# The first of six triangular inverses, made of two blocks of 16 steps joined by small TensorE products

## The chip, the cores and the metric

The program runs on one core of a Trainium2 chip. The metric is the device time in microseconds of one execution, lower is better. Five engines work side by side, each through its own list of instructions: TensorE (PE), VectorE (DVE), ScalarE (ACT), GpSimd (POOL) and SyncE (SP), which here issues all DMAs. They wait for one another through semaphores.

## The reference

```python
# attention: B, H, S, D = 4, 8, 768, 40; state is (B, H, D, D), from zero
for t in range(S):
    y[:, :, t] = einsum('bhd,bhde->bhe', rt, state)
    Sa = einsum('bhde,bhe->bhd', state, at)
    state = state * wt[:, :, None, :] - einsum('bhd,bhe->bhde', Sa, bt) + einsum('bhd,bhe->bhde', vt, kt)
# x = y as (3072, 320); then two dense layers
h = x @ w_in;  solu = h * softmax(h);  ln = (solu - mean) / sqrt(var + 1e-06) * g_ln   # 1024 wide
x = ln @ w_out
h = x @ w_in2; g = max(h, 0) + alpha * min(h, 0);  out = g @ w_out2                  # 2048 wide
```

All in float32. The recurrence is the serial part: each step of the state needs the state before.

## The kernel before

**Tiling.** The 768 time steps are cut into 12 windows of 64 (w) and 24 groups of 32 (g). The 32 heads (4 x 8) lie in the free dimension and in bands of 32 partitions. Inside a group the recurrence is written as matrices: a 32x32 strictly lower matrix L for every head says how each step's correction Sa depends on the earlier ones, and solving for all 32 steps means multiplying with the inverse of a unit lower triangular matrix made of L. One inverse serves four groups (two windows), so there are six; each handles 128 matrices: 4 groups x 32 heads. In the inverse a partition is one matrix's place: the 128 partitions hold four blocks of 32 lanes, and the free dimension holds the 32x32 matrix.

**Phase 1** (`phase1`, line 917). First windows 0 and 1 are loaded and prepared (`prep_load`, `prep_scan`, `prep_kb`, `prep_a`: running products of w on VectorE, applied to k, b, a), and `gen1` (line 314) makes the matrices on TensorE: VectorE copies one half of each PSUM result into XS (line 336), ScalarE copies the other half, negated, into `lraw` (line 339). Then `init` clears tiles on POOL, `load_g(0)` loads the first group, and the first inverse runs alone (lines 941 to 945). After that come 24 slots, one for each group (`slot`, line 844).

**The inverse** (`inverse`, line 343) turns `lraw` into NT by a VectorE transpose of 32x32 blocks (line 366), then takes 31 steps. Step s adds the outer product of column s of L with row s of the result: a product into tmp (line 354) and a sum into M (line 358). In the first inverse VectorE takes the first 10 rows, in two parts, and POOL the rest (`PR`, line 33). A last transpose (line 387) gives NT, which the stages u and uf use as weights. The five later inverses are cut into pieces and put between the other work of the slots (`inv_tasks`, `invs`).

**A slot** runs on TensorE in a written order: `stage_x` (px), then `stage_u` (pu, needs NT), `stage_uf` (pf), `stage_st` (pst; its result goes back to VUS by VectorE, line 482), `stage_g2`, `stage_s` (pss; line 508), `stage_y`, and between them the generation of the next windows, transposes of kbf (`trans`) and pieces of the dense layers. The other engines' order is not written by hand: the framework plans it ahead of time from program order and planned times. `dec` puts the decoding of weight words (`decode`, lines 656 to 665, and the split in lines 692 and 693) behind the last recorded "fence" instruction. The fence is the inverse's last transpose until `stage_st` records its own. Slot 0 decodes the six pieces of the first dense layer.

**Keeping TensorE busy.** `keep(n)` (line 209) issues n products of 128x512 whose result nobody uses. `pace` is called after each little set of products; it counts columns issued lately by planned times, and when the count falls under a floor it puts keep-busy products in until it stands above the floor by a margin. Before the first slot's u stage there are 24 of them at once (`KEEP1`); they wait for one VectorE memset on their operand that is issued after step `KSTEP` of the first inverse.

**SP** issues all loads in one order: the windows, mask, ident, kbf, then the group's tiles (whose targets POOL clears first), window 2, and the first weight words.

Of the kernel before, what the change touches and what calls it, by code (L numbers as in the profile page):

```python
# [7 lines left out]
F32 = mybir.dt.float32  # L8
# [10 lines left out]
WIN = 64  # L19
SPAN = 3.413  # L20
LEVELS = ((3500, 1300), (3100, 1300), (3100, 1300), (3100, 1300))
KEEP0, KEEP1, KSTEP, KEND = 36, 24, 20, 4
PTR, PT0 = (9, 10, 12, 13), (14, 14, 15, 15)
WT = {(0, 'gen00'): 0.44, (0, 'gen20'): 1.8, (0, 'tr1'): 0.19, (0, 'x'): 9.9, (0, 'y'): 0.62, (1, 'tr3'): 2.59, (1, 'u'): 1.48, (1, 'x'): 0.72, (1, 'y'): 1.54, (2, 'tr1'): 0.12, (2, 'u'): 1.34, (3, 'tr3'): 0.38, (3, 'u'): 0.52, (3, 'x'): 0.32, (4, 'tr0'): 0.2, (4, 'tr1'): 0.6, (4, 'u'): 2.76, (5, 'gen30'): 0.32, (5, 'tr3'): 0.38, (5, 'u'): 2.12, (5, 'x'): 0.59, (5, 'y'): 0.25, (6, 'tr0'): 0.2, (6, 'tr1'): 0.58, (6, 'u'): 1.32, (7, 'tr3'): 0.78, (7, 'u'): 0.84, (8, 'tr0'): 0.2, (8, 'tr1'): 0.58, (8, 'u'): 1.28, (9, 'tr3'): 0.9, (9, 'u'): 1.19, (10, 'u'): 2.57, (11, 'u'): 1.09}
VS, NC, NL = 0, (2, 3, 1, 0), (3, 3, 3, 0)
# [21 lines left out]

@with_exitstack
def tile_kernel(ctx: ExitStack, tc: tile.TileContext, w_fm, a0_fm, a_fm, kb_fm, r_fm, v_fm, v_tm,
                w1_in, w1_out, g_ln, w2_in, w2_out, alpha, ident_d, mask_d, r, k, v, w, a, b, w1_nat, out,  # L50
                manual=True):
    nc = tc.nc
    NW = w_fm.shape[0]
# [55 lines left out]
    KBP = [ca.tile([128, 1280], F32, name=f"KBS{i}") for i in range(3)]  # L109
    KBS = [t.rearrange("p (e s d) -> p e s d", e=2, d=D) for t in KBP]  # L110
    XP = ca.tile([128, 320], F32, name="XP")
    LMN = [lm.tile([128, 32, 32], F32, name=f"LMN{i}") for i in range(3)]
    VUS = [ca.tile([128, 2, 16, 40], F32, name=f"VUS{i}") for i in range(2)]
    VUF = [ca.tile([104, 16, 2, 32], F32, name=f"VUF{i}") for i in range(2)]
# [16 lines left out]
    def unit(M, eng):  # L131
        eng.memset(M, 0.0)
        eng.memset(M.rearrange("p a b -> p (a b)")[:, ::33], -1.0)

    def init():
        unit(LMN[0], nc.gpsimd)
        for t in YS:
            nc.gpsimd.memset(t[32:64, 1], 0.0)
            nc.gpsimd.memset(t[0:64, 0], 0.0)
            nc.gpsimd.memset(t[64:128, 1], 0.0)  # L140
        for t in VUS:
            nc.gpsimd.memset(t[32:64, 0], 0.0)
            nc.gpsimd.memset(t[32:64, 1], 0.0)
        for t in VUF:
            nc.gpsimd.memset(t[32:64], 0.0)
        for t in KBS:
            nc.gpsimd.memset(t[32:64, 0], 0.0)
            nc.gpsimd.memset(t[96:128, 1, 0], 0.0)
        for t, i in ((VUS[0], 0), (KBS[0], 1)):
            nc.gpsimd.memset(t[64:128, i], 0.0)  # L150
            nc.gpsimd.memset(t[0:32, 1 - i], 0.0)
        nc.gpsimd.memset(ebias, -float(896 << 23))
        nc.gpsimd.memset(half, -0.5)
        nc.gpsimd.memset(one, 1.0)
# [159 lines left out]
    def gen1(g, half):  # L314
        w, c = divmod(g, 2)
        x = XS[g % 6]
        kbf = st[w]["kbf"]
        if half == 0:
            st["pg1"] = ps_at.tile([128, 8, 2, 32], F32, name="pg", tag="at")
        pg = st["pg1"]  # L320
        wait(st["slot"], "gen%d%d" % (g % 4, half))
        for p in range(half * 4, half * 4 + 4):
            for pe in range(2):
                for i in range(2):
                    o = 64 * pe + 32 * i
                    nc.tensor.matmul(pg[o:o + 32, p], lhsT=kbf[:, pe * 8 + p, c, i, :], rhs=x[0:104, :, pe, p, :],  # L326
                                     start=True, stop=True)
            pace(0.19, 188)
        if half == 0:
            return  # L330
        c4, lraw = g % 4, st["lraw"]
        for e in range(2):
            q = 64 * e
            for pe in range(2):
                o = 64 * pe
                nc.vector.tensor_tensor(out=x[q:q + 32, e, pe], in0=pg[o:o + 32, :, e],
                                        in1=mask[o:o + 32].unsqueeze(1).to_broadcast([32, 8, 32]), op=ALU.mult)
                r = q + 32 * pe
                nc.scalar.activation(out=lraw[r:r + 32, c4 * 8:c4 * 8 + 8, :], in_=pg[o + 32:o + 64, :, e],
                                     func=AF.Copy, scale=-1.0)  # L340


    def inverse(W):
        M, NT = LMN[2 * W % 3], LMN[(2 * W + 1) % 3]

        P = PR[W > 0]

        def rank1(eng, tmp, s, rows):
            nt = 31 - s
            l = NT[:, s + 1:32, s]  # L350
            tv = tmp[:, 0:sum(b - a for a, b in rows) * nt].rearrange("p (i t) -> p i t", t=nt)
            for a, b in rows:
                sh = [128, b - a, nt]
                eng.tensor_tensor(out=tv[:, a - rows[0][0]:b - rows[0][0]], in0=M[:, a:b, s:s + 1].to_broadcast(sh),  # L354
                                  in1=l.unsqueeze(1).to_broadcast(sh), op=ALU.mult)
            for a, b in rows:
                o = M[:, a:b, s + 1:32]
                r = eng.tensor_tensor(out=o, in0=o, in1=tv[:, a - rows[0][0]:b - rows[0][0]], op=ALU.add)  # L358
            return r

        def pool_rows():
            for s in range(P, 31):
                rank1(nc.gpsimd, b1.tile([128, TM], F32, name="tmp2", tag="Yt"), s, [(P, s + 1)])

        def start():
            nc.vector.transpose(out=NT, in_=st["lraw", W].rearrange("p l t -> p t l"))
            if W:
                unit(M, nc.gpsimd)
            pool_rows()

        def step(s):
            n, nt = min(s + 1, P), 31 - s
            m = n // 2
            if n <= SM:
                ops = [(M[:, i, s + 1:32], NT[:, s + 1:32, s], M[:, i, s:s + 1]) for i in range(n)]
            elif nt <= SM:
                ops = [(M[:, 0:n, s + 1 + i], M[:, 0:n, s], NT[:, s + 1 + i, s:s + 1]) for i in range(nt)]
            else:
                st["step"] = rank1(nc.vector, b1.tile([128, 256], F32, name="tmp"), s,
                                   [(0, m), (m, n)] if W == 0 else [(0, n)])  # L380
                return
            for o, x, f in ops:
                st["step"] = nc.vector.scalar_tensor_tensor(out=o, in0=x, scalar=f, in1=o, op0=ALU.mult,
                                                            op1=ALU.add)

        def fin():
            st["fence"] = nc.vector.transpose(out=NT.rearrange("p l t -> p t l"), in_=M.rearrange("p i t -> p t i"))
            st["NT", W] = NT

        yield 1.1, start  # L390
        for s in range(31):
            yield 0.15 + 2 * (s + 1) * (31 - s) / 960.0, (lambda s=s: step(s))
        yield 1.1, fin

    def trans(w, q):
        kbf = st[w]["kbf"]
# [345 lines left out]

    def gen_tasks(w):
        t = [lambda g=g, h=h: gen1(g, h) for g in (2 * w, 2 * w + 1) for h in range(2)]
        if w % 2 == 0:
            first = t[0]
            t[0] = lambda: (new_l(w // 2), first())
        return t

    def new_l(W):  # L750
        st["lraw"] = st["lraw", W] = LMN[2 * W % 3 if W else 2]

    def fill_tasks(g):

# [89 lines left out]
    def slot(g):  # L844
# [33 lines left out]
        if g == 0:  # L878
            st["busy"] = st["idle"]
            keep(KEEP1)  # L880
        stage_u(g)
        nd = (ND if g < 4 else NL if g >= NG - 4 else NC)[g % 4]
        invs(0.2)
# [33 lines left out]
    def phase1():  # L917
        nc.gpsimd.memset(busy, 0.0)
        st["busy"] = ps_w.tile([128, 512], F32, name="busy", tag="w")
        keep(KEEP0)  # L920
        st["slot"] = 0
        init_scan()
        t0, t1 = vec_tasks(0), vec_tasks(1)
        for f in t0[:3]:
            f()
        nc.sync.dma_start(out=mask, in_=mask_d)
        nc.sync.dma_start(out=ident, in_=ident_d)
        for f in t0[3:] + gen_tasks(0) + t1 + gen_tasks(1):
            f()
        with tc.issue_after(st["kb1"].ins):  # L930
            init()
        busy_t = st.pop("busy")
        for q in range(4):
            trans(0, q)
        load_g(0)
        if NW > 2:
            prep_load(2)
            load_a(4)
            load_a(5)
            kb_load(2)  # L940
        for i, (_, f) in enumerate(inverse(0)):
            f()
            if i == KSTEP:
                with tc.issue_after(st["step"].ins):
                    nc.vector.memset(busy[:, 0:1], 0.0)  # L945
        st["idle"] = busy_t
        nc.sync.dma_start(out=gl, in_=g_ln)
        for g in range(NG):
            if g == KEND:
                del st["busy"]  # L950
            slot(g)
        while wts:
            wts.pop(0)()
# [295 lines left out]
    with ExitStack() as ms:  # L1249
# [8 lines left out]


_INS = ['w_fm', 'a0_fm', 'a_fm', 'kb_fm', 'r_fm', 'v_fm', 'v_tm', 'w1_in', 'w1_out', 'g_ln', 'w2_in', 'w2_out', 'alpha',  # L1260
        'ident', 'mask', 'r', 'k', 'v', 'w', 'a', 'b', 'w1_nat']


def _layout(inputs):
# [56 lines left out]
    o['alpha'] = np.asarray(inputs['moe2_alpha']).reshape(-1, 128).T  # L1321
    o['ident'] = np.eye(128, dtype=f32)
    o['mask'] = (np.arange(32)[None, :] > (np.arange(128) % 32)[:, None]).astype(f32)
    for n in 'rkvwab':
        o[n] = np.asarray(inputs[n])
    o['w1_nat'] = words(np.asarray(inputs['moe_w_in']))
# [22 lines left out]
```

## Time and profile before

| | |
|---|---|
| median of 3 runs | 1167.23 us (1165.36 to 1168.53) |
| the profiled execution | 1166.42 us |
| its span in the profile | 1164.6 us |
| PE busy | 978.9 us, 84% |
| DVE busy | 811.2 us, 70% |
| ACT busy | 520.4 us, 45% |
| POOL busy | 503.7 us, 43% |
| share of the chain that ended last | PE 47%, DVE 29%, POOL 7% |

Times in the profile count from the start of the span. Busy shares are averages: up to about 760 us the slots of the recurrence run and VectorE is the busiest engine in most stretches, after that the second dense layer runs on TensorE alone.

### The profile page before, as it was taken

How to read it: one execution, taken by the hardware profiler on the slowest of the kernel's cores; microseconds unless marked ns; L12 is line 12 of the kernel's file. 1: busy time of each engine (PE TensorE's matmuls, PEld its weight loads, DVE VectorE, ACT ScalarE, POOL GpSimd, SP SyncE). 2: the span in 40 equal slices, each digit the busy share in tenths (PEclk: the TensorE clock that was granted, in tenths of full speed). 3: DMA queues.
4: the chain of work that ended last, by engine and by line, in shares of the span. 5: the costliest groups of instructions: out<-in, count | busy, mean ns of one | idle time of the engine just before them, and what ended most of it. 6: DMA issues, size and time to landing. Idle time of an engine off the chain costs nothing.

```text
span 1164.6 us, 37097 instructions
## 1 busy us (share of the span) xinstructions
PE 978.9 (84%) x15934; PEld 808.5 (69%) x15934; DVE 811.2 (70%) x1610; ACT 520.4 (45%) x1198; POOL 503.7 (43%) x546
## 2 busy tenths in 40 slices
PE   7275687588878978888787878889999999999997
PEld 3143354467666767666676667778989999999997
DVE  8898689978997798779977976656533333333343
ACT  3325454476537653755475547556312121212121
POOL 6858455444434442443344234436233333333333
PEclk8687987789888887988888889999999999999999
DMA  7513343334333433343333342443402020201000
GB/s 161 149 53 85 99 137 113 99 104 120 106 97 107 122 80 96 90 100 111 99 85 88 101 135 71 117 141 133 124 2 61 8 62 7 62 6 41 6 23 15
DMA packets 104543, 99.52 MB, mean 85 GB/s; under 512 B 38068, under 2 KB 83764, under 8 KB 104372
## 3 DMA queue, kind: packets, MB, share of 16 engines
q1 hardware_dynamic: 104372, 97.07, 30.6%
q8 instruction: 127, 2.08, 0.8%
q14 instruction: 44, 0.36, 0.1%
HBM read 71.62 MB, written 25.43 MB: 83 GB/s over the span
## 4 chain that ended last, share of the span: by engine, by line
PE 47%; DVE 29%; POOL 7%; issue 6%; ACT 5%; DMA 5%; SPq 0%; POOLq 0%; DVEq 0%; ACTq 0%
PE ph L1015 15%; DVE tmp L354 5%; PE h L575 5%; PE acc L1035 5%; PE acc L1033 5%; PE acc L1034 5%; DVE LMN L358 4%; DMA kbf<-in_kb_fm_dram 4%; DVE VUS L482 2%; DVE KBS L508 2%; PE pf L465 2%; POOL XS L312 2%; DVE H L277 2%; PE po L628 1%; PE pu L442 1%
## 5 line engine op out<-in xcount | busy, mean ns | idle before, releaser
L1022 POOL TENSOR_TENSOR gll<-gt,gh 128x512 fp32r<-128x512 f32 (+1 forms) x112 | 129.0, 1152 | 224.0 <-ACT gh L1021 222.9
L595 DVE TENSOR_SCALAR gt<-ph,al 128x512 f32<-128x512 f32 (+1 forms) x112 | 75.4, 673 | 189.8 <-PE ph L1015 189.6
L1021 ACT CAST gh<-gt 128x512 fp32r<-128x512 f32 (+1 forms) x112 | 62.5, 559 | 254.5 <-DVE gt L596 212.6
L575 PE MATMUL h<-w1h,xt 128*128 128x512 f32 x240 | 105.2, 487 | 16.3 <-ACT h L584 16.3
L312 POOL TENSOR_TENSOR XS<-XS,H 40x512 f32<-40x512 f32 (+1 forms) x48 | 66.6, 1392 | 92.7 <-DVE H L277 55.8
L354 DVE TENSOR_TENSOR tmp<-LMN,LMN 128x87 f32<-128x87 f32 (+25 forms) x189 | 95.0, 514 | 3.4
L1033 PE MATMUL acc<-w2h,gh 128*128 128x320 f32 x288 | 89.0, 309 | 0.0
L1034 PE MATMUL acc<-w2l,gh 128*128 128x320 f32 x288 | 89.0, 309 | 0.0
L1035 PE MATMUL acc<-w2h,gll 128*128 128x320 f32 x288 | 88.9, 309 | 0.0
L528 POOL TENSOR_TENSOR YS<-YS,mask 64x512 f32<-64x512 f32 x48 | 64.0, 1333 | 49.0 <-ACT YS L527 47.2
L211 PE MATMUL busy<-busy 128*128 128x512 bf16 x221 | 66.4, 455 | 19.5 <-DVE busy L945 18.2
L358 DVE TENSOR_TENSOR LMN<-LMN,tmp 128x87 f32<-128x87 f32 (+25 forms) x189 | 76.3, 415 | 2.7
L596 DVE SCALAR_TENSOR_TENSOR gt<-ph,gt 128x512 f32<-128x512 f32 (+1 forms) x112 | 68.8, 615 | 3.7
L575 PE MATMUL h<-w1l,xt 128*128 128x512 f32 x144 | 68.6, 476 | 0.0
L575 PEld LDWEIGHTS h<-w1h,xt 128*128 128x128 f32 x240 | 50.3, 221 | 26.0 <-ACT h L584 18.5
L628 PE MATMUL po<-wo1h,lnh 128*128 128x320 f32 x192 | 67.1, 349 | 0.5 <-DVE lnl L620 0.5
L630 PE MATMUL po<-wo1h,lnl 128*128 128x320 f32 x192 | 61.9, 322 | 0.0
L629 PE MATMUL po<-wo1l,lnh 128*128 128x320 f32 x192 | 61.8, 322 | 0.0
L1015 PE MATMUL ph<-w1h,w2h 128*128 128x512 f32 x180 | 59.3, 394 | 0.0
L211 PEld LDWEIGHTS <-busy 128*128 128x128 bf16 x221 | 22.9, 112 | 49.7 <-DVE busy L945 18.3
L326 PE MATMUL pg<-XS,kbf 104*32 104x64 f32 x1536 | 38.5, 239 | 22.0 <-DVE kbf L303 12.8
L581 ACT ACTIVATE P<-h,sm 128x1024 f32<-128x1024 f32 x24 | 26.7, 1114 | 65.1 <-DVE sm L580 62.1
(200 smaller groups left out, 2743.5 us busy)
## 6 DMA issues: line engine op xcount, KB each, us to landing
kbf<-in_kb_fm_dram SPq DMA_DIRECT2D x24, 416.0 KB
x2d<-x SPq DMA_DIRECT2D x24, 320.0 KB
xd<-Y SPq DMA_DIRECT2D x24, 256.0 KB
xt<-xd SPq DMA_DIRECT2D x12, 512.0 KB
raw<-in_w_in_dram SPq DMA_DIRECT2D x20, 256.0 KB
wt<-in_w_fm_dram SPq DMA_DIRECT2D x24, 211.7 KB
raw<-in_w_in_dram SPq DMA_DIRECT2D x8, 512.0 KB
raw<-in_w_out_dram SPq DMA_DIRECT2D x16, 256.0 KB
```

Source lines behind the costliest of these rows:

```text
L211: nc.tensor.matmul(st["busy"], lhsT=busy[:, 0:128], rhs=busy, start=True, stop=True)
L312: (nc.vector if w < 2 and e in DA else nc.gpsimd).tensor_tensor(out=o, in0=o, in1=h, op=ALU.mult)
L354: eng.tensor_tensor(out=tv[:, a - rows[0][0]:b - rows[0][0]], in0=M[:, a:b, s:s + 1].to_broadcast(sh), in1=l.unsqueeze(1).to_broadcast(sh) ...
L358: r = eng.tensor_tensor(out=o, in0=o, in1=tv[:, a - rows[0][0]:b - rows[0][0]], op=ALU.add)
L575: nc.tensor.matmul(st["h"][:, ns], lhsT=l, rhs=r, start=j == 0, stop=j == len(ops) - 1)
L595: nc.vector.tensor_scalar(out=tmp, in0=h, scalar1=0.0, scalar2=al, op0=ALU.min, op1=ALU.mult)
L628: nc.tensor.matmul(po, lhsT=lh[:, k], rhs=wo1h[:, k], start=k == 0, stop=False)
L1015: nc.tensor.matmul(p, lhsT=l, rhs=r, start=j == 0, stop=j == len(ops) - 1)
L1022: nc.gpsimd.tensor_tensor(out=gll, in0=t, in1=f32(gh), op=ALU.subtract)
L1033: nc.tensor.matmul(acc, lhsT=gh[:, cs], rhs=oh, start=f == 0, stop=False)
L1034: nc.tensor.matmul(acc, lhsT=gh[:, cs], rhs=ol, start=False, stop=False)
L1035: nc.tensor.matmul(acc, lhsT=gll[:, cs], rhs=oh, start=False, stop=f == K2 - 1)
```

## The change

The first inverse is made in another way. With 16x16 blocks, a lower triangular matrix's inverse has the inverses of the two diagonal blocks on its diagonal, and below them a product of three: second inverse, lower left block, first inverse. Both diagonal blocks are inverted side by side in one set of 14 steps, with all 128 partitions as before (VectorE alone, none on POOL). Then TensorE makes the lower left block: `left` multiplies the block with the first inverse, `join` with the second and puts the parts together, one product of 16 or 32 rows for each of the 128 matrices in each (256 products); ScalarE copies between. `join` writes NT for the first four groups. The products stand in slot 0 on TensorE, after the 24 keep-busy products and before stage u, each set of four followed by a call of `pace`.

ScalarE now writes the matrices of the first four groups to GR, columns in reversed order. POOL's `init` no longer clears M of the first inverse but copies three small constants, which come with a triangle in one new input of 128x321. The keep-busy products' memset is issued after step 2, not 20. `dynamic_dma_scratch_size` is set to 1024 and makes room for the new tiles. The last instruction on VectorE of the new inverse, the transpose into VT, is the new fence.

```diff
-KEEP0, KEEP1, KSTEP, KEND = 36, 24, 20, 4
+KEEP0, KEEP1, KSTEP, KEND = 36, 24, 2, 4
...
+    GR = ca.tile([128, 32, 48], F32, name="GR")
+    VR = ca.tile([128, 32, 32], F32, name="VR")
+    VT = ca.tile([128, 32, 16], F32, name="VT")
+    tri = ca.tile([128, 321], F32, name="tri")
...
     def init():
-        unit(LMN[0], nc.gpsimd)
+        for t, c, k in ((GR, 0, 0), (VR, 0, 1), (LMN[2], 16, 2)):
+            i = tri[:, 256 + 16 * k:272 + 16 * k].unsqueeze(1).to_broadcast([128, 32, 16])
+            nc.gpsimd.tensor_copy(out=t[:, :, c:c + 16], in_=i)
...
-                nc.scalar.activation(out=lraw[r:r + 32, c4 * 8:c4 * 8 + 8, :], in_=pg[o + 32:o + 64, :, e],
-                                     func=AF.Copy, scale=-1.0)
+                to = (GR[r:r + 32, c4 * 8:c4 * 8 + 8, 47:15:-1] if g < 4 else
+                      st["lraw"][r:r + 32, c4 * 8:c4 * 8 + 8, :])
+                nc.scalar.activation(out=to, in_=pg[o + 32:o + 64, :, e], func=AF.Copy, scale=-1.0)
...
+    def first_inverse():
+        X, F = LMN[0], LMN[1]
+        L = X[:, 0:16, :].rearrange("p t (b a) -> p b t a", b=2)
+        A = LMN[2]
+        box = {}
+
+        def start():
+            nc.vector.transpose(out=X[:, 15::-1, :], in_=GR[:, :, 32:48].rearrange("p l c -> p c l"))
+            nc.vector.transpose(out=X[:, ::-1, 16:32].rearrange("p s c -> p c s"),
+                                in_=GR[:, :, 16:32].rearrange("p l c -> p c l"))
+
+        def step(s):
+            sh = [128, 2, 15 - s, s]
+            tmp = b1.tile([128, 256], F32, name="tmp")[:, 0:2 * s * (15 - s)]
+            tmp = tmp.rearrange("p (b t a) -> p b t a", b=2, a=s)
+            nc.vector.tensor_tensor(out=tmp, in0=L[:, :, s + 1:16, s:s + 1].to_broadcast(sh),
+                                    in1=L[:, :, s:s + 1, 0:s].to_broadcast(sh), op=ALU.mult)
+            o = L[:, :, s + 1:16, 0:s]
+            st["step"] = nc.vector.tensor_tensor(out=o, in0=o, in1=tmp, op=ALU.add)
+
+        def fin():
+            V = b1.tile([128, 32, 16], F32, name="V", tag="Yt")
+            low = tri[:, 0:256].rearrange("p (t a) -> p t a", a=16).unsqueeze(1).to_broadcast([128, 2, 16, 16])
+            nc.vector.tensor_tensor(out=V.rearrange("p (b t) a -> p b t a", b=2), in0=L, in1=low, op=ALU.mult)
+            nc.vector.memset(V.rearrange("p (b t) a -> p b (t a)", b=2)[:, :, ::17], 1.0)
+            st["fence"] = nc.vector.transpose(out=VT.rearrange("p l a -> p a l"), in_=V.rearrange("p x a -> p a x"))
+            nc.scalar.activation(out=VR[:, :, 31:15:-1], in_=VT, func=AF.Identity, scale=tri[:, 320:321])
+
+        def units(p, lhsT, rhs, rows, ls):
+            for l in ls:
+                for q in range(0, 128, 32):
+                    nc.tensor.matmul(p[q:q + 32, l - ls[0], :], lhsT=lhsT[q:q + rows, l, 0:32], rhs=rhs[q:q + rows, l, :],
+                                     start=True, stop=True)
+                pace(0.042, 16)
+
+        def left(h):
+            if h == 0:
+                box["p"] = ps_at.tile([128, 32, 16], F32, name="pv", tag="at")
+            p = box["p"]
+            units(p[:, 16 * h:16 * h + 16], GR, VT, 16, range(16 * h, 16 * h + 16))
+            if h:
+                nc.scalar.copy(out=A[:, :, 0:16], in_=p)
+
+        def join(h):
+            ls = range(16 * h, 16 * h + 16)
+            p = ps_at.tile([128, 16, 32], F32, name="pn", tag="at")
+            units(p, A, VR, 32, ls)
+            nc.scalar.copy(out=F[:, 16 * h:16 * h + 16, :], in_=p)
+            st["NT", 0] = F
+
+        yield start
+        for s in range(1, 15):
+            yield lambda s=s: step(s)
+        yield fin
+        for f in (left, join):
+            for h in range(2):
+                yield lambda f=f, h=h: f(h)
...
             keep(KEEP1)
+            for f in st["joins"]:
+                f()
         stage_u(g)
...
         nc.sync.dma_start(out=mask, in_=mask_d)
+        nc.sync.dma_start(out=tri, in_=tri_d)
         nc.sync.dma_start(out=ident, in_=ident_d)
...
-        for i, (_, f) in enumerate(inverse(0)):
+        inv = list(first_inverse())
+        st["joins"] = inv[16:]
+        for i, f in enumerate(inv[:16]):
             f()
...
-    nc = _bacc.Bacc("TRN2", target_bir_lowering=False, num_devices=1)
+    nc = _bacc.Bacc("TRN2", target_bir_lowering=False, num_devices=1, dynamic_dma_scratch_size=1024)
```

## Rows read from the trace of the kernel before

**Rows 1.** Stretches: start:end, length, busy us (count) by engine, PEclk, DMA share, GB/s.
```profile
36.00:59.00 23.00, 1.55 (x64) 1.27 (x65) 22.15 (x78) 6.32 (x20) 20.10 (x48) 0.57 0.54 137
68.00:112.00 44.00, 26.73 (x624) 16.51 (x626) 42.88 (x62) 20.07 (x46) 30.89 (x20) 0.79 0.29 83
200.00:400.00 200.00, 159.85 (x3867) 128.46 (x3867) 172.13 (x354) 118.10 (x285) 86.44 (x98) 0.86 0.41 107
```
**Rows 2.** The chain that ended last, 0 to 200 us: start, length, what.
```profile
65.97 2.03 DVE LMN L387
...
120.71 7.58 DMA kbf<-in_kb_fm_dram
```
**Rows 3.** Timeline of VectorE: start, length, line, operation, tiles, shapes, count.
```profile
25.43 0.69 DVE L303 TENSOR_TENSOR kbf<-kbf,F 104x512 f32<-104x512 f32 x1
...
36.13 1.92 DVE L366 STREAM_TRANSPOSE LMN<-LMN 128x1024 f32<-128x1024 f32 x1 [1.19 <-ACT LMN L339]
...
67.85 0.42 DVE L273 TENSOR_SCALAR wc<-wt 104x512 f32<-104x512 f32 x1
...
79.48 1.52 DVE L482 TENSOR_TENSOR VUS<-pst,VUS 40x320 f32<-40x320 f32 x3
...
105.48 0.99 DVE L508 TENSOR_TENSOR KBS<-pss,KBS 40x320 f32<-40x320 f32 x2
```
**Rows 4.** Groups by shape, VectorE, 30 to 66 us: busy us, mean ns, idle before.
```profile
L354 DVE TENSOR_TENSOR tmp<-LMN,LMN 128x29 f32<-128x29 f32 x1 | 0.2, 214 | 0.0
...
L358 DVE TENSOR_TENSOR LMN<-LMN,tmp 128x29 f32<-128x29 f32 x1 | 0.2, 182 | 0.0
```
**Rows 5.** Timeline of VectorE in the second inverse, one product and its sum.
```profile
176.93 0.53 DVE L354 TENSOR_TENSOR tmp<-LMN,LMN 128x207 f32<-128x207 f32 x1
177.49 0.37 DVE L358 TENSOR_TENSOR LMN<-LMN,tmp 128x207 f32<-128x207 f32 x1
```
**Rows 6.** Timeline of TensorE, 39 to 77 us; L211 are the keep-busy products.
```profile
39.53 1.28 PE L429 MATMUL px<-VUS,XS 96*32 96x40 f32 x60 [0.41 <-POOL VUS L151]
59.00 7.29 PE L211 MATMUL busy<-busy 128*128 128x512 bf16 x24 [18.19 <-DVE busy L945]
68.14 0.28 PE L442 MATMUL pu<-XP,LMN 32*32 32x40 f32 x8 [1.85 <-DVE LMN L387]
68.35 1.90 PE L211 MATMUL busy<-busy 128*128 128x512 bf16 x8
70.18 0.72 PE L442 MATMUL pu<-XP,LMN 32*32 32x40 f32 x56
...
72.26 2.12 PE L211 MATMUL busy<-busy 128*128 128x512 bf16 x9
...
74.88 1.42 PE L477 MATMUL pst<-VUS,KBS 64*40 64x40 f32 x64
```
**Rows 7.** Timeline of POOL, 24 to 39 us.
```profile
24.17 2.98 POOL L303 TENSOR_TENSOR kbf<-kbf,F 104x512 f32<-104x512 f32 x2
27.09 0.95 POOL L132 MEMSET LMN<- 128x1024 f32 x1
...
38.86 0.62 POOL L151 MEMSET VUS<- 32x640 f32 x1
```
**Rows 8.** SP: its waits (us, times, longest), and one line of its timeline.
```profile
SPq L418 <- POOL LMN L133: 9.3, 1, 9.3
...
SPq L240 <- PE px L429: 3.7, 1, 3.7
...
44.47 0.99 SPq L688 DMA_DIRECT2D raw<-in_w_in_dram  x2
```
**Rows 9.** Stretches again, for the DMA share and GB/s at the end.
```profile
14.00:20.00 6.00, 4.34 (x14) 1.53 (x14) 5.97 (x7) 3.26 (x8) 3.13 (x4) 0.60 0.89 206
...
50.00:52.00 2.00, 0.00 (x0) 0.00 (x0) 1.97 (x7) 0.00 (x0) 1.76 (x4) 0.50 0.12 45
```
**Rows 10.** Timeline of ScalarE, one instruction of 512 elements.
```profile
39.11 0.72 ACT L251 ACTIVATE H<-wt,lims 104x512 f32<-104x512 f32 x1
```

More of the change, by code (lines that the diff above doesn't have):

```diff
@@ L49, in tile_kernel @@
 def tile_kernel(ctx: ExitStack, tc: tile.TileContext, w_fm, a0_fm, a_fm, kb_fm, r_fm, v_fm, v_tm,
-                w1_in, w1_out, g_ln, w2_in, w2_out, alpha, ident_d, mask_d, r, k, v, w, a, b, w1_nat, out,
+                w1_in, w1_out, g_ln, w2_in, w2_out, alpha, ident_d, mask_d, tri_d, r, k, v, w, a, b, w1_nat, out,
                 manual=True):
@@ L330, in gen1 @@
             return
-        c4, lraw = g % 4, st["lraw"]
+        c4 = g % 4
         for e in range(2):
@@ L744, in gen_tasks @@
         t = [lambda g=g, h=h: gen1(g, h) for g in (2 * w, 2 * w + 1) for h in range(2)]
-        if w % 2 == 0:
+        if w and w % 2 == 0:
             first = t[0]
@@ L750, in new_l @@
     def new_l(W):
-        st["lraw"] = st["lraw", W] = LMN[2 * W % 3 if W else 2]
+        st["lraw"] = st["lraw", W] = LMN[2 * W % 3]
     def fill_tasks(g):
@@ L1260 @@
 _INS = ['w_fm', 'a0_fm', 'a_fm', 'kb_fm', 'r_fm', 'v_fm', 'v_tm', 'w1_in', 'w1_out', 'g_ln', 'w2_in', 'w2_out', 'alpha',
-        'ident', 'mask', 'r', 'k', 'v', 'w', 'a', 'b', 'w1_nat']
+        'ident', 'mask', 'tri', 'r', 'k', 'v', 'w', 'a', 'b', 'w1_nat']
 def _layout(inputs):
@@ L1323, in _layout @@
     o['mask'] = (np.arange(32)[None, :] > (np.arange(128) % 32)[:, None]).astype(f32)
+    tri = np.zeros((128, 256 + 64 + 1), f32)
+    tri[:, :256] = np.tril(np.ones((16, 16), f32), -1).ravel()
+    i16, p = np.eye(16, dtype=f32), np.arange(128) % 32
+    tri[:, 256:272] = np.where(p[:, None] < 16, i16[p % 16], 0)
+    tri[:, 272:288] = -tri[:, 256:272]
+    tri[:, 288:304] = np.where(p[:, None] < 16, 0, i16[15 - p % 16])
+    tri[:, 320] = np.where(p < 16, 0, -1)
+    o['tri'] = tri
     for n in 'rkvwab':
```

## The prediction

> **What bounds the kernel now.** I went from the table by stretches to the chain of waits, then to the order on each engine. The stretches [rows 1] show that from 36 to 59 us VectorE is busy for 22.15 of 23.00 us while TensorE has 1.55 us of work: nearly everything stands behind the first inverse. From 68 to 112 us, the slot of group 0, VectorE is busy for 42.88 of 44.00 us, now with preparing windows, decoding weights and only a little of the recurrence. From 200 to 400 us it still has 86%. The chain [rows 2] runs along VectorE's steps to the last transpose, which ends at 65.97 + 2.03 = 68.00 us, and reaches the load of kbf at 120.71 us. So up to 112 us VectorE's own order is the bound; what matters is when it is through with the inverse, and whether it finds work afterwards. The order [rows 3] shows that: the first transpose starts at 36.13, behind ScalarE's last copy into LMN; at 67.85 preparation follows without a gap, and the first instruction that needs the inverse's result (VUS, line 482) stands at 79.48, 11.5 us behind the transpose; line 508 stands at 105.48.
>
> **The lane, step by step.** Removed: 31.9 us of VectorE (36.13 to 68.00) and POOL's rows beside it. In their place:
> - Two transposes of 512 elements each. The one of 1024 took 1.92 [rows 3]; two halves come to 2.0 (up to 3.8 if a half cost as much as the whole).
> - 14 steps of one product and one sum, on 2·s·(15−s) elements: 28, 52, 72, 88, 100, 108, 112 and back. Single instructions of this kind cost 0.214 + 0.182 at 29 elements [rows 4] and 0.53 + 0.37 at 207, where the sum starts 0.03 after the product's end [rows 5]. Interpolated (1.78 and 1.06 ns an element more) with 0.06 of gaps, the steps cost 0.45, 0.52, 0.58, 0.62, 0.66, 0.68, 0.69 and back: 8.4 us (7.5 without gaps; 10 if short inner runs cost a fifth more).
> - The product with the triangle (512 elements: 0.69, from the product on kbf [rows 3]; up to 1.4), a short memset (0.07) and a transpose of 512 (1.0).
>
> That makes 12.2 us; VectorE is free 31.9 − 12.2 = 19.7 us earlier (18 to 20.5).
>
> The old product reads its column of NT with 128 bytes between elements and costs 0.7 ns an element more than the sum, which reads along rows [rows 4, 5]; the new product reads along rows. [...]
>
> **What stands in front of it.** The triangle's load is 128 × 321 × 4 = 164 KB, ahead of ident and kbf in SP's queue. From 14 to 20 us the DMA engines move 206 GB/s at 0.89 busy [rows 9], so all that follows lands 164/206 = 0.8 us later, and both VectorE and POOL need kbf there: 0.8 us, between 0 (gaps take it up) and 1.2 (with 0.4 of issue). ScalarE's reversed write into GR has no row; only its last one is on the path: between 0 and 0.4 (its own length doubled); I take 0, since it moves as many elements.
>
> **POOL, SP and the weight words.** POOL sets 128x1024 (0.95) and a diagonal less and makes three copies of 512 elements. A copy lies between half that memset (0.5) and POOL's two-operand product (1.49 [rows 7]); with 0.8, nearer the memset, POOL's list grows by 3·0.8 − 1.1 = 1.3 us (0.4 to 3.4). That list releases px (VUS, line 151, at 38.86 [rows 7]) and SP (9.3 us of wait on it, then 3.7 us on px [rows 8]), so px ends at 40.81 + 0.8 + 1.3 = 42.9 and the words issued at 44.47 leave 2.1 later. They had landed by about 50.3 (45 GB/s left in 50 to 52 [rows 9]); the first of them now lands near 50. VectorE is free at 36.13 + 0.8 + 12.2 = 49.1 and wants it as its second instruction: I take 1.0 us of waiting (0 to 3).
>
> **The join.** The 24 keep-busy products start after step 2 and after px, at 42.9, and last 7.3 [rows 6], to 50.2; so the join starts 1.1 after the transpose into VT. It is 256 products. The u stage's 56 of 32x32 took 0.72 [rows 6], 12.9 ns each: 3.3 us. The pacing rule adds to it: counted by the kernel's own constants, 8 keep-busy products stand after lane 0 and 9 after lane 20 of the second half; eight took 1.90 and nine 2.12 [rows 6]. With ScalarE's copy out of PSUM between (0.72 for 512 elements [rows 10] and 0.1 of signals, an estimate), u starts 3.3 + 1.9 + 2.1 + 0.8 = 8.1 us after the join's start; before, 0.14 after the inverse. Then u 0.8 (its own eight are the eight above), uf 1.9 (70.90 to 74.88 less its nine), nine keep-busy 2.1, half of st 0.7: 13.6; eight more keep-busy and the other half, 16.2. Before, both halves were done 8.3 after the inverse [rows 6].
>
> The rows show 12.9 ns from product to product on the four bands of 32 rows. [...]
>
> **What is late next.** VectorE reaches line 482 after 11.5 us of other work. The operands come 1.1 + 13.6 = 14.7 and 17.3 us after its transpose. In the old order it waits 3.2, does two instructions (1.0) and waits 1.6 again: 4.8 us, less what it can pull forward (lines 660 and 662 of the second decode, 1.4) and part of the wait for words that is already counted: 3.0 (0 to 9). The rest of the recurrence is covered: line 508 stands 26 us behind line 482.
>
> **Sum.** 19.7 − 0.8 − 1.0 − 3.0 = 14.9 us. From there on every slot hangs on the one before, so I carry it whole to the end: 1166.42 − 14.9 = 1151.5 for the profiled execution, whose time is 0.8 under the median of 1167.23. Forecast: 1152. Its own range, from the bounds above: 12 to 18 us gained, 1149 to 1155.
>
> **Rivals.**
> - *All of it.* The other engines' order is planned anew; if preparation and further decoding fill the 3.0 and the 1.0, 19 us are gained: 1148. For it: over 30 us of other work stand in the slot. Against: decoding is tied to fences in st, and the next window's load begins only when VectorE gives its buffers back.
> - *The join's chain takes the bound.* If slot 0 hangs on TensorE's chain, count from the end of st: 76.3 before, 50.2 + 16.2 = 66.4 after, 10 us gained: 1157. For it: half of what the lane saves is paid back in one chain. Against: VectorE at 97% in that slot.
> - *POOL's list waits for ScalarE.* The copy into GR stands at the head of POOL's list, and ScalarE writes the same tile till 36.1. If it waits for that, the list starts 9 us later, px ends at 51.9, the join starts at 59.2 and u at 67.3: 1 us gained, 1166, no change. Against: columns 0 to 16 aren't ScalarE's, and on kbf two engines worked on interleaved halves of a tile at once (POOL 24.17 to 27.15, VectorE at 25.43 [rows 3, 7]).
> - *Slower: the new plan costs in every slot.* The order on VectorE, ScalarE and POOL is set ahead of time from planned times. If the shift in slot 0 makes the planner put a dependent instruction too early in the later slots, as line 482 behind the join, VectorE waits in each. With 22 slots left and 1.5 us in each (half of the 3.0 above), 33 us are lost against 14.9: 1185. It decides from 14.9/22 = 0.7 us a slot; from 0.85 on it is slower by over 0.3%. For it: with 86% busy there is little room to catch up. Against: inside a later slot nothing moves against anything else.
>
> **Chances.** The forecast 0.56, all of it 0.16, the join's chain 0.17, POOL's list 0.05, slower 0.06. About 0.3% (3.5 us) is what a measurement can tell from no change. Faster is the first three, 0.89; the same 0.05; slower 0.06. The range 1146 to 1159 takes in the first three with their bounds and leaves out the last two and the tails.
>
> **What would show it.** Right: the transpose into VT ends near 49 us, 12 us after the lane's first; 28 products and sums of 0.2 to 0.4 us; 17 keep-busy products inside the join; line 482 near 62 to 64 us after a wait of some 3 us; the load of kbf of 120.71 near 106. Wrong: POOL's first memset later than 31 us, a transpose of 512 at 2 us, u later than 61 us, or a gain at 125 us that is smaller at 760 us.

## The result and the profile after

The changed kernel takes 1153.18 us (median of 7 runs, 1147.26 to 1155.45), the kernel before 1165.36 (7 runs, the three of the table before among them, 1157.87 to 1168.53): a ratio of 0.9896 [0.9866, 0.9925], 12.2 us or 1.0% faster. The forecast was 1152 in 1146 to 1159. The profiled execution of after took 1147.26 us, the lowest of its seven, and that of before 1166.42: the pair of traces differs by 19 us, the medians by 12. Single executions of one kernel scatter by up to 11.4 us about their median (e11), so traces are compared stage by stage here and kernels by medians.

The page of after, busy time and instructions by engine:

```profile
PE 975.0 (85%) x16433; PEld 812.2 (71%) x16456; DVE 788.2 (69%) x1527; ACT 524.6 (46%) x1202; POOL 484.3 (42%) x505
```

The stretches of after that answer to [rows 1]; columns as there:

```profile
36.00:59.00 23.00, 13.38 (x395) 7.79 (x396) 21.50 (x53) 8.79 (x25) 9.96 (x20) 0.77 0.55 135
68.00:112.00 44.00, 36.98 (x952) 24.90 (x959) 30.92 (x53) 24.58 (x59) 31.98 (x27) 0.92 0.37 109
200.00:400.00 200.00, 164.60 (x4021) 134.34 (x4020) 166.71 (x343) 117.35 (x285) 84.25 (x97) 0.89 0.40 105
```

Between 68 and 112 us VectorE now has 30.92 us of work instead of 42.88: what stood there has moved ahead. The timeline of VectorE, after (line 411 answers to 366, 549 to 482, 575 to 508, 723 to 656):

```profile
35.73 1.04 DVE L411 STREAM_TRANSPOSE LMN<-GR 128x512 f32<-128x512 f32 x1 [1.20 <-ACT GR L347]
...
41.81 0.27 DVE L419 TENSOR_TENSOR tmp<-LMN 128x112 f32<-128x112 f32 x1
42.12 0.27 DVE L422 TENSOR_TENSOR LMN<-LMN,tmp 128x112 f32<-128x112 f32 x1
...
46.58 1.08 DVE L429 STREAM_TRANSPOSE VT<-V 128x512 f32<-128x512 f32 x1
47.55 0.40 DVE L279 TENSOR_SCALAR wc<-wt 104x512 f32<-104x512 f32 x1
...
59.82 1.10 DVE L723 TENSOR_SCALAR wem<-raw 128x512 int32<-128x512 int32 x1
...
72.47 1.01 DVE L549 TENSOR_TENSOR VUS<-pst,VUS 40x320 f32<-40x320 f32 x2
74.97 0.99 DVE L549 TENSOR_TENSOR VUS<-pst,VUS 40x320 f32<-40x320 f32 x2 [1.49 <-PE pst L544]
```

The lane lasts from 35.73 to 47.66, 11.9 us instead of 31.9 [rows 3]. Behind it stand 24.8 us of other work up to the first VUS (before: 11.5), preparation of window 3 ahead of the decoding, which starts only at 59.82. VectorE then waits once on the way through line 549, 1.49 us.

TensorE, after (line 435 is the join's products, 217 the keep-busy ones, 509 stage u):

```profile
42.41 6.51 PE L217 MATMUL busy<-busy 128*128 128x512 bf16 x23 [0.33 <-DVE LMN L422]
48.85 0.25 PE L435 MATMUL pv<-VT,GR 16*32 16x16 f32 x8
49.03 1.90 PE L217 MATMUL busy<-busy 128*128 128x512 bf16 x8
50.86 1.56 PE L435 MATMUL pv<-VT,GR 16*32 16x16 f32 x164
54.25 0.89 PE L435 MATMUL pv<-VT,GR 16*32 16x16 f32 x84 [1.83 <-issue]
55.84 0.85 PE L435 MATMUL pn<-VR,LMN 32*32 32x32 f32 x44 [0.70 <-ACT LMN L445]
59.35 1.92 PE L435 MATMUL pn<-VR,LMN 32*32 32x32 f32 x124 [2.66 <-issue]
61.60 1.14 PE L217 MATMUL busy<-busy 128*128 128x512 bf16 x3 [0.33 <-issue]
63.35 1.25 PE L217 MATMUL busy<-busy 128*128 128x512 bf16 x5 [0.61 <-issue]
64.54 0.92 PE L435 MATMUL pn<-VR,LMN 32*32 32x32 f32 x86
65.31 0.50 PE L509 MATMUL pu<-XP,LMN 32*32 32x40 f32 x33
```

The join is 512 records, two for each float32 product, and holes put down to "issue" stand between them: from its first record to u 16.4 us pass, where 8.1 were forecast.

### The profile page after: what moved, and what is told of

Same layout as the page of the kernel before. It is cut to its first block, busy times and chain, and to the rows that moved or that the text cites. A ratio compares the mean times of both kernels' runs of the same rounds, so it can differ in the third digit from the quotient of the medians.

```text
span 1145.5 us, 38002 instructions
## 1 busy us (share of the span) xinstructions
PE 975.0 (85%) x16433; PEld 812.2 (71%) x16456; DVE 788.2 (69%) x1527; ACT 524.6 (46%) x1202; POOL 484.3 (42%) x505
## 4 chain that ended last, share of the span: by engine, by line
PE 48%; DVE 28%; ACT 8%; POOL 6%; issue 5%; DMA 4%; SPq 1%; POOLq 0%; DVEq 0%; ACTq 0%
PE ph L1087 15%; PE acc L1107 5%; PE acc L1106 5%; PE acc L1105 5%; DVE tmp L361 5%; PE h L642 4%; DVE LMN L365 3%; DMA kbf<-in_kb_fm_dram 2%; DVE VUS L549 2%; DVE KBS L575 2%; PE pf L532 2%; DVE P L649 1%; DVE H L283 1%; PE py L607 1%; PE ptr L681 1%
## 5 line engine op out<-in xcount | busy, mean ns | idle before, releaser
L1094 POOL TENSOR_TENSOR gll<-gt,gh 128x512 fp32r<-128x512 f32 (+1 forms) x112 | 127.8, 1141 | 224.8 <-ACT gh L1093 223.5
L361 DVE TENSOR_TENSOR tmp<-LMN,LMN 128x87 f32<-128x87 f32 (+8 forms) x135 | 83.4, 618 | 2.6
L642 PEld LDWEIGHTS h<-w1h,xt 128*128 128x128 f32 x240 | 51.1, 224 | 28.7 <-ACT h L651 18.9
L217 PE MATMUL busy<-busy 128*128 128x512 bf16 x208 | 57.4, 423 | 6.2 <-issue 4.4
L365 DVE TENSOR_TENSOR LMN<-LMN,tmp 128x87 f32<-128x87 f32 (+8 forms) x135 | 59.5, 440 | 2.6
L732 POOL TENSOR_TENSOR dec<-em 128x256 f32<-128x256 f32 x36 | 31.4, 874 | 60.4 <-DVE em L729 32.0
L342 DVE TENSOR_TENSOR XS<-pg,mask 32x256 f32<-32x256 f32 x96 | 39.8, 415 | 23.4 <-ACT LMN L347 19.9
```

The costliest lines, as they stand in the source:

```text
L642: nc.tensor.matmul(st["h"][:, ns], lhsT=l, rhs=r, start=j == 0, stop=j == len(ops) - 1)
L1094: nc.gpsimd.tensor_tensor(out=gll, in0=t, in1=f32(gh), op=ALU.subtract)
```

## The experiments

Three theories were tested. One: the join's chain on TensorE bounds slot 0. Its rival: VectorE's own list bounds it, and what stands on TensorE beside it is free up to some length. And a third, on the slots after it: the order that the framework plans for VectorE, ScalarE, POOL and SP came out different, and costs in the later slots. In the built programs the last 1450 and more of VectorE's some 1850 instructions stand in one of two orders, row for row: the **old order** is that of before, the **new order** that of after. ScalarE, POOL and SP split in the same two ways; TensorE's order behind slot 0 is the same in all. All runs in one table, in us. "Yt" is the start of stage y's result on VectorE in slot 0, "rest" the time from slot 3's to slot 23's, "8 to 9" that from slot 8's to slot 9's, all of the profiled execution; the time is the median, the ratio that to before. The experiments ran on three chips (e1 to e4, e5 to e8, e9 to e12), each ratio against executions of before on the same chip.

| kernel | order | u starts | Yt | rest | 8 to 9 | time | ratio |
|---|---|---|---|---|---|---|---|
| before | old | 68.1 | 110.9 | 563.0 | 34.5 | 1165.36 | |
| after | new | 65.3 | 92.1 | 564.2 | 38.4 | 1153.18 | 0.9896 [0.9866, 0.9925] |
| e1_again | new | 67.2 | 98.6 | 570.9 | 38.6 | 1153.09 | 0.9869 [0.9845, 0.9893] |
| e2_no_join | old | 51.3 | 91.1 | 559.7 | 34.1 | 1146.94 | 0.9833 [0.9806, 0.9861] |
| e3_join_twice | new | 83.0 | 111.0 | 567.1 | 38.1 | 1171.64 | 1.0025 [0.9999, 1.0051] |
| e4_no_steps | new | 66.9 | 92.2 | 567.9 | 39.1 | 1151.67 | 0.9851 [0.9822, 0.988] |
| e5_one_pass | new | 58.9 | 93.2 | 571.3 | 38.4 | 1153.36 | 0.9905 [0.9871, 0.9938] |
| e6_no_pace | old | 63.4 | 93.5 | 564.0 | 34.2 | 1145.9 | 0.9829 [0.9786, 0.9872] |
| e7_neither | old | 49.3 | 85.6 | 559.5 | 33.7 | 1142.42 | 0.98 [0.9754, 0.9845] |
| e8_u_first | its own | 52.8 | 97.0 | 574.1 | 37.2 | 1157.64 | 0.992 [0.9894, 0.9945] |
| e9_busy8 | old | 63.8 | 92.3 | 561.4 | 34.8 | 1148.83 | 0.9864 [0.9827, 0.99] |
| e10_busy12 | new | 62.6 | 93.1 | 565.4 | 39.3 | 1155.91 | 0.9923 [0.9895, 0.9952] |
| e11_u_first_no_pace | old | 51.4 | 94.3 | 563.4 | 34.6 | 1152.53 | 0.9871 [0.9828, 0.9913] |
| e12_no_pace_again | old | 62.0 | 92.2 | 560.1 | 33.6 | 1145.57 | 0.9835 [0.9798, 0.9872] |

**e1: the changed kernel again**, with no edit.

> The changed kernel once more, for a second profile and a better interval. The first pair of profiles differs by 19 us, the medians by 12. Theory A (the gain of slot 0 is 20 us in every execution, and later slots give some back in most of them): slot 0's Yt again near 92 us, the second inverse's first transpose again some 20 us before the old one, and the loss to the median between 200 and 760 us. Rival B (slot 0 itself varies): slot 0's Yt later than 95 us in an execution of 1153 us. Time 1150 to 1156 by both, ratio to before 0.987 to 0.992.

The gain stands (15.0 us against before on that chip), but this profiled execution was 14.5 us longer than the other: 6.5 in slot 0 and 6.7 from slot 3 on. Nine keep-busy products in it took 4.02 us, near what they take before at a granted clock of 0.50 (seven in 3.17 us, from 80.17 to 83.34); at 1.00 nine took 2.12 there [rows 6]. So the expected 92 us did not come back, and the rival is right in so far as slot 0 itself varies; a single trace of one kernel can be 6 us off in either part.

**e2: no join.**

```diff
-        for f in (left, join):
+        def plain():
             for h in range(2):
-                yield lambda f=f, h=h: f(h)
+                nc.scalar.copy(out=F[:, :, 16 * h:16 * h + 16], in_=VR[:, :, 16:32])
+            st["NT", 0] = F
+        yield plain
```

> Leaves out the 256 products, their keep-busy products and the copy of the lower left block: two ScalarE copies from VR fill NT, so that the lane stands alone and u can start some 15 us earlier. Theory V (VectorE's queue sets slot 0, and the planner puts other work under the join): time within 4 us of the changed kernel, 1149 to 1153. Rival J (the chain join, u, uf, st sets slot 0): 12 to 16 us less, 1137 to 1141.

With u 14.0 us earlier, slot 0 gained only 1.0 us. So VectorE's list is as long as the join's chain there. Yet the median fell by 6 us, outside both ranges, and most of that lies behind slot 0, where this program has the old order.

**e3: the join twice.**

```diff
-                    nc.tensor.matmul(...)
+                    for _ in range(2):
+                        nc.tensor.matmul(...)
```

> Issues each of the join's products twice, so TensorE's chain before u grows by about 10 us (512 more records at the 13 ns of the u stage, plus what their issue costs). Theory V: part of it is covered by work that VectorE pulls forward, 2 to 7 us more than the changed kernel. Rival J: all of it shows, 10 to 14 us more, 1163 to 1167.

u came 17.7 us later and Yt 18.9: past the present length, everything that the join takes shows, as the rival had it. The chain grew by more than the 10 us expected, and the median by 18.5 instead of 10 to 14. TensorE's timeline of this kernel shows the holes at a fixed distance:

```profile
56.02 1.41 PE L436 MATMUL pv<-VT,GR 16*32 16x16 f32 x128 [2.02 <-issue]
61.67 1.97 PE L436 MATMUL pv<-VT,GR 16*32 16x16 f32 x128 [4.24 <-issue]
66.22 1.46 PE L436 MATMUL pv<-VT,GR 16*32 16x16 f32 x84 [2.58 <-issue]
68.35 0.90 PE L436 MATMUL pn<-VR,LMN 32*32 32x32 f32 x44 [0.68 <-ACT LMN L446]
69.67 2.00 PE L436 MATMUL pn<-VR,LMN 32*32 32x32 f32 x128 [0.42 <-issue]
73.12 2.02 PE L436 MATMUL pn<-VR,LMN 32*32 32x32 f32 x128 [1.45 <-issue]
```

**e4: only two of the 14 steps.**

```diff
-            yield lambda s=s: step(s)
+            yield lambda s=s: step(s) if s < 3 else None
```

> Leaves out steps 3 to 14 of the lane (24 VectorE instructions, 6.9 us); keep-busy products and join stay where they are, so TensorE's join can start no earlier than the end of keep-busy near 49 us. Theory V: VectorE is free 6.9 us earlier and the time falls by 4 to 7 us, to 1146 to 1149. Rival J: the join's start is held by the keep-busy products, the time stays within 2 us of 1153.

Nothing in slot 0, as the rival had it: the join still started at 48.65, held by the keep-busy products ahead of it, and u at 66.9. The lane alone is not the bound any more.

**e5: one pass for each product of the join.**

```diff
-  lhsT=lhsT[q:q + rows, l, 0:32], rhs=rhs[q:q + rows, l, :],
+  lhsT=lhsT[q:q + rows, l, 0:32].bitcast(BF16)[:, 1::2], rhs=rhs[q:q + rows, l, :].bitcast(BF16)[:, 1::2],
```

> The join's operands are read as the upper halves of their words (bf16), so that each of the 256 products is one pair of weight load and product instead of two; values are truncated. Theory I (the gaps of 'issue' on TensorE in the join come because dense streams of small products run out of instructions, about one gap for each 128 pairs): the gaps in the join fall from some 6 us to under 3, and the stretch from the first pv to the first pu from 16.4 to 18 us to 8 to 10. Rival P (each gap has to do with the products themselves, their operands or the pacing): gaps as before, stretch 13 us or more. Time by both at best what leaving the join out gave: 1148 to 1153.

TensorE's timeline of this kernel, from the first record on:

```profile
48.76 0.19 PE L435 MATMUL pv<-VT,GR 16*32 16x16 bf16 x4
...
50.71 1.14 PE L435 MATMUL pv<-VT,GR 16*32 16x16 bf16 x124
52.59 0.48 PE L435 MATMUL pn<-VR,LMN 32*32 32x32 bf16 x44 [0.74 <-ACT LMN L445]
54.49 0.45 PE L435 MATMUL pn<-VR,LMN 32*32 32x32 bf16 x40 [1.41 <-issue]
```

Half the records and one large hole instead of two: u 10.2 us after the join's first record instead of 16.4. That is the sign of theory I, and rival P is out. Slot 0 gained nothing from it, and the new order stayed, and with it the time.

**e6 and e12: no keep-busy products inside the join**, the same program twice.

```diff
                                      start=True, stop=True)
-                pace(0.042, 16)
```

> No call of pace in the join, so the 17 keep-busy products (4 to 6 us) fall out of it. Theory I: issue is the limit, the gaps grow by what the keep-busy products covered, and the stretch from the first pv to the first pu falls by 2 us at most, from 16.4 to 18 to some 15 to 17. Rival P: it falls by all of the 4 to 6 us, to 11 to 13. Time 1151 to 1156.

> The join without pace once more, beside the three others, for an interval: 1144 to 1149 by theory C, 0.980 to 0.985 of the kernel before; slots 4 to 23 in 559 to 565 us.

u came only 2 to 3 us earlier, though 16 products of 4.3 us went. The stretch from the first pv to the first pu is 14.5 us in e6, between the two expectations, and 12.9 in e12, as rival P had it. The holes of the join grew from 5.4 to 7.0 us in e6 and not at all in e12 (5.4), so theory I's forecast holds in part only. Seven keep-busy products now stand inside u instead. TensorE's timeline of e6:

```profile
48.88 1.69 PE L435 MATMUL pv<-VT,GR 16*32 16x16 f32 x180
52.76 1.25 PE L435 MATMUL pv<-VT,GR 16*32 16x16 f32 x76 [2.18 <-issue]
54.69 0.96 PE L435 MATMUL pn<-VR,LMN 32*32 32x32 f32 x52 [0.68 <-ACT LMN L444]
57.04 1.93 PE L435 MATMUL pn<-VR,LMN 32*32 32x32 f32 x128 [1.39 <-issue]
62.41 1.23 PE L435 MATMUL pn<-VR,LMN 32*32 32x32 f32 x74 [3.44 <-issue]
```

Slot 0 stayed as it was, but the order is the old one, and the kernel is the fastest complete one: 1145.9 and 1145.57, some 7 us below the changed kernel's medians (0.4 to 0.7% by the ratios) and 1.7% below before.

**e7: no steps and no join**, the edits of e2 and e4 together.

> Leaves out both steps 3 to 14 of the lane and the join (two copies fill NT). Apart, they gave 2 us and 4 us against the changed kernel at 1153. Theory B (two chains of nearly one length, VectorE's work and lane-join-u, each covers the other): together more than the sum, 8 to 11 us, 1142 to 1145. Rival S (slot 0 has another bound, loads or POOL): the sum or less, 1147 to 1150.

Slot 0 gained 6.5 us, where each edit alone gave at most 1.0. The two chains, VectorE's through the lane and its list, and TensorE's through the join, are of nearly one length there; only shortening both makes slot 0 shorter. The median is in theory B's range, but not by slot 0 alone: 6 us came already with e2's old order, and by slot 3 the trace has given the rest back (Yt at 187.8, against 188.7 in e2 and 187.4 in after), and the intervals of the ratios of e2 and e7 overlap.

**e8 and e11: u of the first lanes first**, e11 also without `pace`. `left` and `join` were cut into lanes 0 to 7, all that group 0 needs, ahead of u, and the rest after `stage_g2`:

```diff
-            for f in st["joins"]:
+            for f in st["joins"][:2]:
...
+        if g == 0:
+            for f in st["joins"][2:]:
+                f()
```

> The whole computation, in another order: the join for lanes 0 to 7 alone (64 products) ahead of stage u, the other 24 lanes after stage_g2 of slot 0, where TensorE waited for ScalarE and VectorE. If the join's chain is exposed by the 4 us that leaving it out gave: 2 to 4 us less than the changed kernel, 1149 to 1151. If the rest now stands in front of s and y: no gain, 1152 to 1156.

> Lanes 0 to 7 joined first, the rest after stage_g2, and no pace in the join; the later slots' plan is that of the kernel before. u starts near 51 to 53 us. If slot 0 hangs on VectorE alone there: as without pace, 1144 to 1148. If the first part of the recurrence was exposed: 1141 to 1145. If the rest of the join stands in the way of s and y again: 1147 to 1151.

u started 12.5 and 13.9 us earlier and Yt was later. In e8 the deferred products stand before stage s on TensorE, which waits there for ScalarE's copy between `left` and `join`:

```profile
70.34 0.44 PE L435 MATMUL pv<-VT,GR 16*32 16x16 f32 x29 [2.15 <-issue]
...
81.64 2.12 PE L435 MATMUL pn<-VR,LMN 32*32 32x32 f32 x139 [6.89 <-ACT LMN L442]
...
87.15 0.49 PE L565 MATMUL pss<-KBS,VUS 64*40 64x40 f32 x8
```

A better place for them was not tried. e11 has the old order and lies between: 1152.53, above all three ranges expected; its six executions spread from 1141 to 1154.

**e9 and e10: the order alone.** No `pace` in the join, but 8 or 12 keep-busy products before its last part; by the built programs 8 leaves the old order, 12 gives the new one.

```diff
-                pace(0.042, 16)
...
-            for f in st["joins"]:
+            for i, f in enumerate(st["joins"]):
+                if i == 3:
+                    keep(8)
```

> Pace is out of the join, and 8 keep-busy products stand before its last part. The plan of VectorE, ScalarE, POOL and SP for the later slots is then row for row that of the kernel before. Theory C (besides slot 0, the changed kernel loses some 6 us in slots 4 to 23, because the engines' order there was planned otherwise than in the kernel before, on a TensorE order that is the same): 1145 to 1149, slots 4 to 23 in 559 to 565 us by Yt, and slot 9 in 34 us. Rival N (nothing but noise in the later slots): as the changed kernel, 1151 to 1155.

> The same with 12 instead of 8 keep-busy products, 0.9 us more of TensorE in slot 0; with that the plan of the later slots is row for row that of the changed kernel. Theory C: 5 to 7 us more than with 8, 1151 to 1155, slots 4 to 23 in 564 to 572 us and slot 9 in 38 us. Rival N: 0 to 2 us more than with 8.

Four more products on TensorE, 0.9 us by [rows 6] (nine in 2.12), and Yt in slot 0 is 0.8 us apart; the medians are 7.1 us apart, 0.9864 [0.9827, 0.99] against 0.9923 [0.9895, 0.9952]: the intervals overlap by 0.0005 only, and on the one chip five of e9's six executions are below the lowest of e10's twelve. So the order costs. One place of it shows in the traces: slot 9. SP's timeline there in e9 (old order), where slot 8's Yt starts at 339.82:

```profile
349.84 0.33 SPq L236 DMA_DIRECT2D kbf<-in_kb_fm_dram  x1
353.06 0.36 SPq L782 DMA_DIRECT2D od<-dec  x1
353.51 0.59 SPq L715 DMA_DIRECT2D x2d<-x  x1
354.15 0.60 SPq L236 DMA_DIRECT2D kbf<-in_kb_fm_dram  x1
```

The same in e10 (new order), with slot 8's Yt at 344.85:

```profile
357.54 0.36 SPq L746 DMA_DIRECT2D raw<-in_w_out_dram  x1
358.40 0.34 SPq L782 DMA_DIRECT2D od<-dec  x1
358.84 0.59 SPq L715 DMA_DIRECT2D x2d<-x  x1
359.52 1.21 SPq L236 DMA_DIRECT2D kbf<-in_kb_fm_dram  x2
```

In the old order kbf's first half leaves 10.0 us after Yt, ahead of two writes of results; in the new one 14.7 us after it, behind the writes and one more load of words. VectorE's instructions on kbf there that wait for the load, in e9:

```profile
360.22 2.28 DVE L309 TENSOR_TENSOR kbf<-kbf,F 104x512 f32<-104x512 f32 x2 [0.52 <-DMA kbf<-in_kb_fm_dram]
```

And in e10:

```profile
365.70 1.29 DVE L309 TENSOR_TENSOR kbf<-kbf,F 104x512 f32<-104x512 f32 x2 [3.00 <-DMA kbf<-in_kb_fm_dram]
368.11 2.28 DVE L309 TENSOR_TENSOR kbf<-kbf,F 104x512 f32<-104x512 f32 x2 [1.11 <-DMA kbf<-in_kb_fm_dram]
```

3.6 us more of waiting for this load, in a slot that is 4.5 us longer. It is so in every run of the two orders: with the old order slot 9 takes 33.6 to 34.8 us and waits at most 0.69 for this load, with the new one 38.1 to 39.3 and 2.9 to 4.1. Slot 9 is not the only place: on the means of the same runs slot 4 takes 2.9 us more in the new order (42.9 against 40.0, without overlap), while slots 10 and 11 together take 3.0 less, so that much of what slot 9 loses is given back right behind it.

## Why the prediction was right, and where not

The total was right, the way to it in several steps not. By its steps:

- **Lane:** 12.2 us forecast, 11.9 found; the steps 7.7 instead of 8.4. At 112 elements product and sum both take 0.27: the product's extra 0.7 ns an element, which the sum had kept, is gone. The new product reads along rows, but no run changes the reading of the column alone, and in the second inverse of before a product with pieces of 3 elements of such a column cost no more than its sum (line 354 at 213.49 us and line 358 at 213.78, 87 elements, 0.25 us each), so the reason stays open.
- **In front of it:** the triangle's 0.8 us did not show; the lane began 0.4 us earlier than before. POOL's three copies took 1.46, 0.61 and 0.80, 2.9 instead of 2.4, beginning at 26.60: no wait for ScalarE, so that rival is out.
- **The join, the mis-sized term:** 256 × 12.9 ns = 3.3 us forecast, 6.6 us found. The count of 56 in [rows 6] was of records, and a float32 product is two (stage u issues 32 products and shows 64 records); the join is 512 records, 12.9 ns each on the mean. By the product it is 26 ns, twice what the sum had taken; e5's products of one record took 9.2 ns each (124 in 1.14 us). On top came 5.4 us of "issue", for which the sum had no term; all but 0.3 of it ends 1.4 to 1.5 us behind a packet of a queue named "instruction" (last section). In all 16.4 us instead of 8.1, less 1.3 for an earlier start: u at 65.3, past the 61 that I had put down as a sign of being wrong.
- **Waits of VectorE:** 1.0 for words and 3.0 at line 482 forecast; none and 1.5 found, in spite of the later u. The rival "All of it" had this right: the planner filled the gap, 24.8 us of other work instead of 11.5, and the first VUS stood at 72.47 instead of near 62 to 64. So the transpose into VT ended 20.3 us earlier and slot 0 18.8 earlier instead of 14.9 (12.3 in e1; 17.4 to 18.7 in e5, e6, e9, e10 and e12, which leave the steps and the join's products in place). e2, e3 and e7 show how near it was: the join's chain is just covered, and one longer by a few us would show whole.
- **"I carry it whole to the end" is the step that failed.** The rival that the new plan costs in every slot, given 0.06, came true in small. The profiled pair does not show it: there "rest" is 564.2 against 563.0, and the gain of 18.8 is still 19.3 at slot 23. In e1 it falls from 12.3 to 4.7. Over the profiled runs "rest" is 561.6 us on the mean of seven with the old order and 567.8 on that of six with the new one (by the table's column; e8 is in neither): 6.2 us, without overlap, and e9 against e10 has 7.1 in the medians. 18.8 − 6.2 = 12.6 is near the 12.2 of the medians, though the 18.8 is of one pair of executions. It is not 1.5 us in each of 22 slots, as the rival had it: slots 4 and 9 lose 2.9 and 4.4 (38.7 against 34.2 on the mean in slot 9), others gain and lose less; in slot 9 a load is issued later.

So 14.9 came out nearly right by luck: some 4 us too little in slot 0 and 6 us too much behind it cancelled, and in slot 0 the join's missing 8 us were hidden under VectorE's list. What stays open: why the planned order tips between 8 and 12 keep-busy products, and what lengthens slot 4 in the new order. That kbf's place in SP's queue is the cause in slot 9 is read from the traces; moving that load alone was not tried.

## What to carry to other kernels

When a framework plans the order of several engines, a change in one stage can change the order everywhere after it: compare the planned orders of the two programs first, and look stage by stage whether a gain is kept. When two chains of nearly one length meet, each alone looks free; test them by shortening both, and see whether the gain lasts. And before a row's count is used as a count of operations, divide it by the operations that the code issues.

## What the runs showed of the hardware

The join's streams of small products are held up by "issue": in e3 holes of 0.4 to 4.2 us stand 128 records apart, in e6 and e12 of 0.8 to 3.4. e5, with half the records, has one of 1.41 where after has two of 1.83 and 2.66. In all of these the first of the holes stands behind TensorE's 180th record from the join's first (keep-busy products counted), whether the records are of float32 products or, as in e5, of bf16 ones.

The DMA records of the traces set the holes beside a queue, q8, that the page of after names "instruction". It has 131 packets of 16 KB there; TensorE's products and weight loads are 32,889, 251 for each packet:

```profile
q8 instruction: 131, 2.15, 0.8%
```

In after, packets of this queue end at 52.79, 57.83, 62.00 and 65.67 us, and holes of "issue" end at 54.25, 59.35, 63.35 and 67.08: all four of 0.4 us or more between 44 and 95 us, each 1.4 to 1.5 us behind a packet. From 95 to 760 us six of after's seven such holes end 1.4 to 1.6 us behind one, the other 4.6; before has none from 44 to 95 us, and from there to 760 eight of nine end 1.3 to 1.6 us behind one, the other 4.4. In e11 seven keep-busy products are the 137th to 143rd record from the join's first, and from 48 to 68 us there is no hole of "issue" above 0.2 us. No run changed these packets; that TensorE waits for its instructions in the holes is a reading of the traces.

The granted clock from 68 to 112 us rose from 0.79 to 0.92 on the mean; single stretches of before have 0.50 (48 to 59 us) and 1.00 (68 to 72). From 36 to 59 us TensorE had only 1.55 us of work before [rows 1], and 13.38 after; whether the one follows from the other was not tested. Before, nine keep-busy products took 2.12 us at 1.00 [rows 6] and seven took 3.17 at 0.50, from 80.17 to 83.34.
